# Decode attention over two layers: K fetched by pairs of heads into alternating slots, one loop turn per pair

## Chip, cores and metric

The kernel runs on one core of one Trainium2 chip. The metric is device time in microseconds (us) of one launch. TensorE is called PE, VectorE DVE, ScalarE ACT, GpSimd POOL and SyncE SP, as in the profile.

## What is computed

One token for each of two sequences (B = 2) passes two layers, each an attention over cached K and V and a gated mixer with an MLP. The attention is nearly all of the work:

```python
q = (x @ wq).reshape(B, Sq, H, Dh)                       # H = 32 heads, Dh = 128
scores = einsum("bhqd,bhkd->bhqk", q, k_cache) * Dh**-0.5 # Sk = 16384 keys per head
p = softmax(scores)
o = einsum("bhqk,bhkd->bhqd", p, v_cache)
x = x + o.reshape(B, Sq, H * Dh) @ wo
```

All arrays are bf16. K and V of one head are 4 MB each; there are U = 64 heads (B times H), and both layers read all of them. The last heads of layer 0 (61 to 63) stay on chip and come first in layer 1.

## The kernel before

**Memory.** SBUF holds one tensor `mem` of six slots, each 32768 bytes in each of 128 partitions: one slot for K or V of a head. `plan_all` (L516) writes down, in order, every transfer and the slot it goes to. SP issues them strictly in that order (L99 to L101): a transfer waits until the last readers of its slot are done, and all that stand behind it wait with it.

**The loop.** Most heads go in pairs through a hardware loop on PE, ACT and DVE: heads 1 to 60 in layer 0, 58 heads in layer 1 (`ENTER`, `LEAVE`, L347). K of the pair's first head has a slot, K of the second another, and V of both is one transfer into two neighbouring slots (`plan_pair`, L445), whose row is 65536 bytes for each partition. K comes in rows of 32768 bytes. In layer 0 two of the six slots are not used while the loop runs.

**One head.** A head's K lies as 128 blocks of 128 keys. Half of them are scored on PE: `transposes` (L1292) turns eight blocks (a chunk) into PSUM `tps`, ACT copies the chunk to `kt` (`evacuate`, L1310), and `scores` (L1317) multiplies it with the column of q. PE does the scores two chunks behind the transposes. The other half is scored on DVE: `dots` (L1340) multiplies 16 blocks with a row of q spread over the partitions and sums (L1348, L1354). Softmax takes the maximum on DVE, over the partitions by POOL's `partition_all_reduce` (L1370), and exp on ACT (L1382, L1385).

**A pair.** V of a pair puts head 0 on partitions 0 to 63 and head 1 on 64 to 127, but p of each head lies on all 128. So `spread_p` (L1407) redistributes p of each head by two matmuls, ACT copies the halves to `both` (L1424), and `pv_pair` (L1445) runs 256 matmuls with two columns each (L1455). Within one turn the order is: first head, second head with the softmax of the first inside, softmax of the second, PV of both, ACT's copy of the result to `o_acc` (L1459).

**Tokens.** That a transfer has landed is told to PE and DVE by POOL, in its own order (`relay`, L81; emitted at L205), between its reductions.

Of the kernel before, what the change touches and what calls it, by code (L numbers as in the profile page):

```python
# [32 lines left out]
class Graph:  # L33
# [10 lines left out]
    def __init__(self, nc):  # L44
        self.nc = nc
        self.ops = {e: [] for e in self.ENGS}
        self.all = []
        self.writer = {}
        self.readers = {}
        self.dma_sems = {}  # L50
        self.dma_count = {}
        self.loops = {e: {} for e in self.LOOPED}

# [55 lines left out]
    def loop(self, first, turns):  # L109

        for e, i in first.items():
            n = len(self.ops[e]) - i
# [21 lines left out]
    def emit(self):  # L134
# [76 lines left out]
        def runner(e):  # L211
            def run(eng):
# [3 lines left out]
                while i < len(ops):  # L216
                    if i in self.loops.get(e, ()):
                        n, turns = self.loops[e][i]
                        taken = self._turn(eng, ops, i, n, turns, taken, wait, needs, emit_op, handle)
# [15 lines left out]
    def _turn(self, eng, ops, first, n, turns, taken, wait, needs, emit_op, handle):  # L235
# [22 lines left out]
        with self.nc.Fori(0, turns, 1, engines=OrderedEngineSet([me]), head_slot={me: 0}) as turn:  # L258
            seen = {}
            for i in range(n):  # L260
# [3 lines left out]
            for k, v in step.items():  # L264
                eng.sem_inc(handle(k), -v)
        return {**taken, **{k: taken.get(k, 0) + v * turns for k, v in step.items()}}
# [65 lines left out]
class KB:  # L332
    NL = 2
    CH = 8
# [12 lines left out]
    ENTER = (1, 3)  # L347
    LEAVE = (61, 61)
# [28 lines left out]
    def _alloc(self):  # L377
# [14 lines left out]
        self.both_keys = [("qb", 0), ("p", 0), ("p2", 0), "both"]  # L392
        self.s_dve = [sb(f"s_dve{i}", [128, 2 * (self.BP - self.PB)], FP32) for i in range(self.NS)]
        self.q_f = sb("q_f", [128, U], FP32)
        self.q_col = sb("q_col", [128, self.NS], BF16)
        self.mx = sb("mx", [128, 5, self.NS], FP32)
        self.ls = sb("ls", [128, 2, self.NS], FP32)
        self.l = sb("l", [128, U], FP32)
# [46 lines left out]
    def plan_pair(self, u, slot):  # L445

        v = self.V.rearrange("b h s d -> (b h s d)")
        n = self.NB * 128 * 128
        self.store.plan(("w", u, 0, 2 * self.NB), "pair", slot * self.TILE, 2 * self.TILE,
                        [(lambda m: m, v[u * n:(u + 2) * n].rearrange("(p x) -> p x", p=128))])  # L450

# [64 lines left out]
    def plan_all(self):  # L516
# [10 lines left out]
        self.plan_tile("k", 0, 1)  # L527
# [5 lines left out]
        for t, u, slot in (("k", third, 1), ("k", third + 1, 3), ("v", third, 4), ("k", third + 2, 5),  # L533
                           ("v", third + 1, 0), ("v", third + 2, 2)):
# [22 lines left out]
        o, a, z = self.order(1), self.ENTER[1], self.LEAVE[1]  # L557
        assert a == self.CARRY + 1 and z == U - 3
        for s in range(a, z, 2):
            self.plan_tile("k", o[s], 3, (quarter, half, half + quarter) if s == a else ())  # L560
            self.plan_tile("k", o[s + 1], 5)
            if s == a:
                self.plan_tile("k", o[z], 0)
            self.plan_pair(o[s], 1)
        self.plan_tile("k", o[z + 1], 4)
        self.plan_tile("k", o[z + 2], 3)
        self.plan_tile("v", o[z], 5)
        self.plan_tile("v", o[z + 1], 1)
        self.plan_tile("v", o[z + 2], 2, (half,))
        self.cuts["wo", 1] = [(i, j, 4 * T + i * row) for i, j in ((0, 11), (11, 22), (22, 32))]  # L570
        at = 4 * T + 32 * row
        ats = [at, at + w3r, at + 2 * w3r, 0, w3r]
        assert at + 3 * w3r <= 6 * T
        w4_at = w3r + w3r // 2
# [3 lines left out]
        assert w4_at + 16 * row <= T and w1_at + 5 * row <= 4 * T  # L578
# [31 lines left out]
    def build(self):  # L610
# [8 lines left out]
        self.pool(lambda e: e.memset(self.both[:, 1, :], 0.0), writes=["both"])  # L619
# [354 lines left out]
    def attention(self, l):  # L974
        U, LEAD, NS = self.U, self.LEAD, self.NS
        self.l_now = l
        o = self.order(l)
        pend = []
        enter, leave = self.ENTER[l], self.LEAVE[l]
        turns = (leave - enter) // 2  # L980
# [601 lines left out]
```

## Time and profile before

| | us |
|---|---|
| median of three runs (2546.06 to 2546.59) | 2546.34 |
| the profiled execution, whole | 2545.75 |
| its span, first to last instruction | 2543.9 |
| DVE busy | 1875.3 |
| PE busy | 1588.5 |
| ACT busy | 1250.8 |
| HBM read | 1092.37 MB, 429 GB/s over the span |

The slices of the page give each engine's busy share and the DMA engines' in 40 equal pieces of the span; the chain follows the work that ended last back to what released it. A row of waits names who waited, for whom, how long in total, how often and the longest. Instructions that only set registers, branch or change semaphores are not counted as busy; they are shown when a line is asked for, with a q behind the engine's name.

### The profile page before, as it was taken

The numbers are of one execution on the slowest core, as the hardware profiler recorded it, in microseconds if no ns is written. First come the engines' busy times: TensorE is split into PE (matmuls) and PEld (weight loads), VectorE is DVE, ScalarE is ACT, GpSimd is POOL, SyncE is SP. The second block draws the span as 40 slices with busy tenths as digits, with TensorE's granted clock in tenths as the row PEclk, the third lists the DMA queues.
The fourth block names the chain that finished last, engine by engine and source line by source line (L and its number), as shares of the span: only waits on it lengthen the run. The fifth ranks groups of instructions, "written<-read, shape, count | busy, mean of one in ns | idle before, by whom it ended". The sixth has DMA issues, their size and how long they took to land.

```text
span 2543.9 us, 75560 instructions
## 1 busy us (share of the span) xinstructions
PE 1588.5 (62%) x34642; PEld 1520.1 (60%) x34642; DVE 1875.3 (74%) x1811; ACT 1250.8 (49%) x2114; POOL 109.6 (4%) x154
## 2 busy tenths in 40 slices
PE   3656666566566566565776656656656666566566
PEld 3555656566565565565765656656556566566566
DVE  5787787777877877877748687787787787777884
ACT  3454555554544544545535455454454555554553
POOL 0000000000000000000000000000000000000000
PEclk8666665565656656666656566566666565665665
DMA  9999999999999999999999999999999999999999
GB/s 414 424 437 429 434 438 430 428 442 424 434 433 432 432 437 428 436 435 426 418 413 432 434 429 437 429 431 439 425 435 433 431 436 433 428 437 430 432 431 383
DMA packets 38432, 1093.19 MB, mean 430 GB/s; under 512 B 4196, under 2 KB 5352, under 8 KB 11496
## 3 DMA queue, kind: packets, MB, share of 16 engines
q1 hardware_dynamic: 38376, 1092.39, 99.9%
q8 instruction: 41, 0.67, 0.1%
q14 instruction: 15, 0.12, 0.0%
HBM read 1092.37 MB, written 0.00 MB: 429 GB/s over the span
## 4 chain that ended last, share of the span: by engine, by line
DMA 60%; DVE 27%; PE 7%; issue 4%; ACT 1%; POOL 0%; SPq 0%; POOLq 0%; DVEq 0%; ACTq 0%
DMA mem<-in_A_k_cache_dram 57%; DVE s_dve L1354 17%; DVE prod L1348 9%; PE tps L1298 3%; DMA mem<-in_B_w_dram 1%; DMA mem<-in_A_v_cache_dram 1%; PE mps L1482 1%; PE sps L1328 1%; PE sps L1263 1%; DVE diag L1259 1%; ACT mem L1314 0%; PE mps L897 0%; PE mps L1455 0%; DMA mem<-in_A_wq_dram 0%; DMA mem<-in_A_wo_dram 0%
## 5 line engine op out<-in xcount | busy, mean ns | idle before, releaser
L1354 DVE TENSOR_REDUCE s_dve<-prod 128x16 f32<-128x2048 bf16 x504 | 1151.1, 2284 | 13.3
L1314 ACT ACTIVATE kt<-tps 128x1024 bf16<-128x1024 bf16 x992 | 966.5, 1029 | 171.8 <-PE tps L1298 159.9
L1348 DVE TENSOR_TENSOR prod<-mem,qb 128x2048 bf16<-128x2048 bf16 x492 | 602.1, 1224 | 524.5 <-POOLq L205 490.6
L1298 PE MATMUL tps<-same,mem 128*128 128x128 bf16 x8192 | 910.7, 285 | 31.3 <-issue 24.6
L1298 PEld LDWEIGHTS tps<-same,mem 128*128 128x128 bf16 x8192 | 730.8, 130 | 37.2 <-issue 30.2
L1455 PEld LDWEIGHTS mps<-both,mem 128*128 128x128 bf16 x15104 | 407.5, 103 | 48.2 <-ACT both L1424 43.2
L1455 PE MATMUL mps<-both,mem 128*128 128x2 bf16 x15104 | 412.5, 165 | 32.6 <-ACT both L1424 27.8
L1328 PE MATMUL sps<-q_col,kt 128*128 128x1 bf16 x7936 | 364.6, 168 | 53.6 <-ACT kt L1314 44.9
L1328 PEld LDWEIGHTS sps<-q_col,kt 128*128 128x128 bf16 x7936 | 351.7, 108 | 74.2 <-ACT kt L1314 69.6
L1418 PE MATMUL sps<-p,same 128*128 128x128 bf16 x236 | 46.3, 299 | 481.2 <-ACT p L1385 481.2
L1418 PEld LDWEIGHTS sps<-p,same 128*128 128x128 bf16 x236 | 15.6, 111 | 491.2 <-ACT p L1385 491.2
L1263 PE MATMUL sps<-diag,same 128*128 128x128 bf16 x126 | 36.0, 286 | 286.4 <-DVE diag L1259 284.6
L1370 POOL PARTITION_ALL_REDUCE mx<-mx x128 | 106.5, 832 | 2366.3 <-DVE mx L1368 2259.0
L1459 ACT ACTIVATE o_acc<-mps 128x2 f32 x59 | 10.2, 172 | 383.7 <-PE mps L1455 383.7
L1263 PEld LDWEIGHTS sps<-diag,same 128*128 128x128 bf16 x126 | 13.1, 104 | 296.8 <-DVE diag L1259 290.1
L1379 ACT ACTIVATE mx<-mx 128x1 f32<-128x1 f32 x128 | 26.2, 205 | 332.1 <-POOL mx L1370 332.0
L1266 ACT ACTIVATE qb<-sps 128x128 bf16<-128x128 f32 x123 | 33.8, 275 | 228.1 <-PE sps L1263 228.1
L1424 ACT ACTIVATE both<-sps 64x256 bf16<-64x256 f32 x118 | 44.6, 378 | 57.2 <-PE sps L1418 57.2
L1365 DVE TENSOR_REDUCE mx<-sps 128x1 f32<-128x64 f32 x128 | 28.2, 220 | 23.2 <-PE sps L1328 23.1
L1382 ACT ACTIVATE p<-s_dve,mx 128x64 bf16<-128x64 f32 x123 | 42.8, 348 | 4.0
L1314 ACT ACTIVATE mem<-tps 128x1024 bf16<-128x1024 bf16 x32 | 31.3, 1044 | 18.1 <-PE tps L1298 16.0
L1430 ACT ACTIVATE l<-ls 128x1 f32 (+1 forms) x120 | 35.3, 294 | 9.0
(131 smaller groups left out, 460.5 us busy)
## 6 DMA issues: line engine op xcount, KB each, us to landing
mem<-in_A_k_cache_dram SPq DMA_DIRECT2D x124, 4096.0 KB, 24.0
mem<-in_A_v_cache_dram SPq DMA_DIRECT2D x5, 4096.0 KB, 29.7
mem<-in_B_w_dram SPq DMA_DIRECT2D x21, 576.0 KB, 7.8
mem<-in_B_w_dram SPq DMA_DIRECT2D x7, 1152.0 KB, 32.7
mem<-in_A_v_cache_dram SPq DMA_DIRECT2D x3, 2048.0 KB, 36.9
mem<-in_A_wq_dram SPq DMA_DIRECT2D x10, 512.0 KB, 6.5
mem<-in_A_wo_dram SPq DMA_DIRECT2D x8, 576.0 KB, 18.4
mem<-in_A_wq_dram SPq DMA_DIRECT2D x4, 1024.0 KB, 8.0
```

Source lines behind the costliest of these rows:

```text
L1263: self.pe(lambda pe: pe.matmul(qps, lhsT=self.ones_bf[:, :], rhs=self.diag[:, :], start=True, stop=True, skip_group_check=True), reads=["o ...
L1298: ins = pe.transpose(self.tps[t][:, j * 128:(j + 1) * 128], buf[:, j * 128:(j + 1) * 128], self.ident[:, :])
L1314: self.act(lambda e: e.activation(out=out, in_=self.tps[t][:, :], func=ACT.Copy), reads=[("tps", t)], writes=keys, sig=("evac", c, t, k))
L1328: ins = pe.matmul(self.sps[sp][:, c * self.CH + j:c * self.CH + j + 1], lhsT=buf[:, j * 128:(j + 1) * 128], rhs=self.q_col[:, sp:sp + 1], ...
L1348: self.dv(lambda e: e.tensor_tensor(out=prod, in0=buf.rearrange("p (j d) -> p j d", d=128), in1=qbc, op=ALU.mult), reads=[("qb", r)] + key ...
L1354: self.dv(lambda e: e.tensor_reduce(out=sd[:, c0:c0 + DB], in_=prod, axis=AX.X, op=ALU.add), reads=["prod"], writes=[("s_dve", r)], sig=(" ...
L1370: self.pool(lambda e: e.partition_all_reduce(mx[3], mx[2], channels=128, reduce_op=ROP.max), reads=[("mx2", i), "cleared"], writes=[("mx3" ...
L1382: self.act(lambda e: e.activation(out=p[:, n:self.NB], in_=self.s_dve[i][:, 0:self.NB - n], func=ACT.Exp, bias=mx[4], scale=self.scale, ac ...
L1418: ins = pe.matmul(out[:, h * n:(h + 1) * n], lhsT=lhsT, rhs=self.p[i][:, :], start=True, stop=True, skip_group_check=True)
L1424: self.act(lambda e: e.activation(out=self.both[lo:hi, k, :], in_=out[lo:hi, :], func=ACT.Copy), reads=[("sps", 0), ("qps", 0)], writes=se ...
L1430: self.act(lambda e, c: e.activation(out=self.l[:, bass.ds(c, 1)], in_=self.ls[:, 0, i:i + 1], func=ACT.Identity, bias=self.ls[:, 1, i:i + ...
L1455: ins = pe.matmul(self.mps[:, 448:450], lhsT=buf[:, b * 128:(b + 1) * 128], rhs=self.both[:, :, col], start=b == 0, stop=b == 2 * self.NB ...
```

## The change

K of a pair is now one transfer like V, `kk`, into two neighbouring slots, alternately at two places: slots 0 and 1 or 2 and 3 in layer 0, slots 0 and 1 or 4 and 5 in layer 1 (`KK`). V of a pair, `vv`, has one place: slots 4 and 5, or 2 and 3. All six slots are in use. With K and V of a pair in one layout, both heads' K stands on its own half of the partitions throughout: scores have two columns, one max and one reduction serve both heads, and exp is written by four activations, each on 64 partitions, right where PV reads it; `spread_p` goes. PV of a pair is done one turn later, behind the scores of the next pair. A turn of the loop is one pair at one of the two places, so within the loop PE and DVE compute the place from the turn (`moved`). The first pair of each layer is written out ahead of the loop. Layer 1 enters the loop's heads one later (`ENTER` 4), so that one single head goes ahead of them, with its PV, and two come behind.

```diff
@@ class Graph, _turn
+            self.moved = (turn + 1) % 2 * self.shift[eng_name][first]
@@ class KB
-    ENTER = (1, 3)
-    LEAVE = (61, 61)
+    ENTER = (1, 4)
+    LEAVE = (61, 62)
+    KK = ((0, 2), (0, 4))
+    VV = (4, 2)
+    def plan_pairs(self, l):
+        o = self.order(l)
+        firsts = [o[s] for s in range(self.ENTER[l], self.LEAVE[l], 2)]
+        for i, u in enumerate(firsts):
+            self.plan_pair("kk", u, self.KK[l][i % 2])
+            if i:
+                self.plan_pair("vv", firsts[i - 1], self.VV[l])
+        return firsts[-1]
@@ plan_all
-        for u in range(1, third, 2):
-            self.plan_tile("k", u, 0)
-            self.plan_tile("k", u + 1, 2)
-            self.plan_pair(u, 4)
+        last = self.plan_pairs(0)
+        self.plan_tile("k", third, 1)
+        self.plan_pair("vv", last, self.VV[0])
...
+        s = self.ENTER[1] - 1
+        self.plan_tile("k", o[s], 3, (quarter, half, half + quarter))
+        self.plan_tile("v", o[s], 2)
+        last = self.plan_pairs(1)
@@ attention
+        self.single(l, s, ahead)
+        self.softmax_max(l, s, o[s])
+        self.softmax_exp(l, s, o[s])
+        self.landed(l, "v", o[s])
+        for g in range(4):
+            self.pv(l, s, o[s], g)
+        self.keep_by_act(l, s)
+        self.pool(lambda e: e.memset(self.both[64:, 0, :], 0.0), writes=[*self.both_keys, "cleared"])
+        firsts = [o[s] for s in range(enter, leave, 2)]
+        for i, u in enumerate(firsts):
+            if i == 1:
+                first = self.g.mark()
+                self.base = self.chunk
+            self.pair(l, i, u, firsts[i - 1] if i else None)
+        a, z = self.KK[l]
+        self.g.loop(first, len(firsts) - 1, (z - a) * self.TILE // 2)
@@ new
+    def pair(self, l, i, u, was):
+        n, CH, DB, NB = 4 * self.PB // self.CH, self.CH, self.DB, self.NB
+        nm = ("kk", u, 0, 2 * NB)
+        buf, keys = self.store.buf(nm), self.store.keys(nm)
+        base = self.KK[l][0] * self.TILE // 2
+        self.g.relay("tensor", keys, [("landed", nm)])
+        self.g.relay("vector", keys, [("seen", nm)])
...
+        def place(b, m):
+            if self.g.moved is None:
+                return buf[:, b * 128:(b + m) * 128]
+            return self.mem[:, bass.ds(self.g.moved + (base + b * 128), m * 128)]
...
+                    ins = pe.transpose(self.tps[t][:, j * 128:(j + 1) * 128], place(c * CH + j, 1), self.ident[:, :])
...
+                    ins = pe.matmul(self.sps[0][:, 2 * b:2 * b + 2], lhsT=kt[:, j * 128:(j + 1) * 128],
+                                    rhs=self.q_col2[:, :], start=True, stop=True, skip_group_check=True)
...
+        for c in range(n):
+            turned(c, self.chunk)
+            self.evacuate(c, self.chunk)
+            pend.append((c, self.chunk))
+            self.chunk += 1
+            while len(pend) > self.LEAD:
+                score(*pend.pop(0))
+            if c % 2 == 0:
+                dot(c // 2)
+            if c == n // 2 and was is not None:
+                self.pair_l(was)
+        while pend:
+            score(*pend.pop(0))
+        if was is not None:
+            self.pair_pv(was)
+        self.pair_q(keys)
+        self.used(l, nm, 2 * NB)
...
+        self.pool(lambda e: e.partition_all_reduce(self.mx2[:, 4:6], self.mx2[:, 2:4], channels=128, reduce_op=ROP.max),
+                  reads=["mx2_2", "cleared"], writes=["mx2_4"])
+        self.pair_column(u + 2)
...
+        for part in (1, 0):
+            for h, (lo, hi) in enumerate(sides):
+                src = self.s_dve2[lo:hi, :] if part else self.half_scores(h)
+                self.act(lambda e, h=h, lo=lo, hi=hi, src=src, part=part: e.activation(
+                    out=self.both[lo:hi, h, NB * part:NB * (part + 1)], in_=src, func=ACT.Exp,
...
+    def pair_pv(self, u):
+        nm = ("vv", u, 0, 2 * self.NB)
+        buf, keys = self.store.buf(nm), self.store.keys(nm)
+        self.g.relay("tensor", keys, [("landed", nm)])
+        n = 2 * self.NB // 4
+        for g in range(4):
+            def f(pe, g=g):
+                for b in range(g * n, (g + 1) * n):
+                    ins = pe.matmul(self.mps[:, 448:450], lhsT=buf[:, b * 128:(b + 1) * 128], rhs=self.both[:, :, b],
+                                    start=b == 0, stop=b == 2 * self.NB - 1, skip_group_check=True)
+                return ins
+            self.pe(f, reads=self.both_keys + [("landed", nm)] + keys, writes=["ops"], sig=("w", g))
+        self.act(lambda e, c: e.activation(out=self.o_acc[:, bass.ds(c, 2)], in_=self.mps[:, 448:450], func=ACT.Copy),
+                 reads=["ops"] + keys, writes=["o_acc"], sig="keep_pair", col=u)
+        self.used(0, nm, 2 * self.NB)
```

`single` does one head as the code before did, without a loop; `pair_q`, `pair_diag` and `pair_column` make the rows and columns of q for the next pair, and `pair_l` keeps the sums of exp.

Two places of the order. SP at the start of the program before, from K and V of head 0 on; 128x16384 is one head, 128x32768 a pair, and the wait is for the readers of the slot (PE is `done_tensor`, ACT `done_scalar`):

```order
L101 DMA mem<-in_A_k_cache_dram 128x16384
L101 DMA mem<-in_A_v_cache_dram 128x16384
L101 DMA mem<-in_A_k_cache_dram 128x16384 x2
L101 DMA mem<-in_A_v_cache_dram 128x32768 [waits done_tensor]
L101 DMA mem<-in_A_k_cache_dram 128x16384 [waits done_tensor] x2
L101 DMA mem<-in_A_v_cache_dram 128x32768 [waits done_scalar]
```

The same place of SP's queue now:

```order
L103 DMA mem<-in_A_k_cache_dram 128x16384
L103 DMA mem<-in_A_v_cache_dram 128x16384
L103 DMA mem<-in_A_k_cache_dram 128x32768
L103 DMA mem<-in_A_k_cache_dram 128x32768 [waits done_tensor]
L103 DMA mem<-in_A_v_cache_dram 128x32768
L103 DMA mem<-in_A_k_cache_dram 128x32768 [waits done_tensor]
L103 DMA mem<-in_A_v_cache_dram 128x32768 [waits done_scalar]
```

The first V pair has moved behind the second K pair, and from then on each K pair stands ahead of the V pair of the pair before it.

PE in a turn of the loop of layer 0 before, from its entry; `tps<-same,mem` are transposes, `sps<-q_col,kt` scores, L258 is the loop's own line:

```order
L258 UNCONDITIONAL_BRANCH
L1298 MATMUL tps<-same,mem 128x128 [waits landed_tensor_tensor]
L1298 MATMUL tps<-same,mem 128x128 x23
L1328 MATMUL sps<-q_col,kt 128x1 [waits scalar_tensor]
L1328 MATMUL sps<-q_col,kt 128x1 x7
L1298 MATMUL tps<-same,mem 128x128 x8
```

PE at the end of a turn of the same loop now, from the middle of its last chunk (ISA is a register instruction, L1260 is PV, `sps<-diag` and `sps<-p` spread the next rows of q):

```order
L1142 ISA
L1142 MATMUL tps<-same,mem 128x128
L1153 MATMUL sps<-q_col,kt 128x2 [waits scalar_tensor]
L1153 MATMUL sps<-q_col,kt 128x2 x7
L1153 MATMUL sps<-q_col,kt 128x2 [waits scalar_tensor]
L1153 MATMUL sps<-q_col,kt 128x2 x7
L1153 MATMUL sps<-q_col,kt 128x2 [waits scalar_tensor]
L1153 MATMUL sps<-q_col,kt 128x2 x7
L1260 MATMUL mps<-both,mem 128x2 [waits landed_tensor_tensor]
L1260 MATMUL mps<-both,mem 128x2 x255
L1228 MATMUL sps<-diag,same 128x128 [waits vector_tensor]
L1228 MATMUL sps<-p,same 128x128
```

Each transpose inside the loop now has a register instruction ahead of it, and PV stands behind the scores of the next pair instead of its own.

More of the change, by code (lines that the diff above doesn't have):

```diff
@@ L233, in emit, with _turn @@
                     sect(runner(e))
-    def _turn(self, eng, ops, first, n, turns, taken, wait, needs, emit_op, handle):
+    def _turn(self, eng, eng_name, ops, first, n, turns, taken, wait, needs, emit_op, handle):
         table = [[needs(ops[first + t * n + i]) for i in range(n)] for t in range(turns)]
@@ L1245, in landed @@
             self.g.relay("tensor", keys, [("landed", nm) for nm in some])
-            if both:
-                self.g.relay("vector", keys, [("seen", nm) for nm in some])
     def q_column(self, u, s):
@@ L1253, in q_column, with q_row @@
                 reads=["q_f"], writes=[("q_col", i)], sig=("qc", i), col=u)
-    def q_row(self, u, s, bank=None, ahead=False):
+    def q_row(self, u, s, bank=None, after=()):
         i = self.ix(self.l_now, s)
```

357 lines of the change are left out of this document (181 added, 176 removed).

## The prediction

> **What bounds the kernel now.** I read the page first: its slices, its DMA part and its chain.
>
> ```profile
> span 2543.9 us, 75560 instructions
> PE 1588.5 (62%) x34642; PEld 1520.1 (60%) x34642; DVE 1875.3 (74%) x1811; ACT 1250.8 (49%) x2114; POOL 109.6 (4%) x154
> DMA  9999999999999999999999999999999999999999
> q1 hardware_dynamic: 38376, 1092.39, 99.9%
> DMA 60%; DVE 27%; PE 7%; issue 4%; ACT 1%; POOL 0%; SPq 0%; POOLq 0%; DVEq 0%; ACTq 0%
> ```
>
> No engine is over 74%, and the transfers fill every slice: they take 99.9% of the span. The DVE share of the chain is therefore no bound by itself; it is what stands between two transfers of one slot. Next I read a turn of the loop, and a long stretch of turns, in the table by windows.
>
> ```profile
> 411.00:449.80 38.80, 23.57 (x521) 22.62 (x519) 29.29 (x27) 19.27 (x34) 1.66 (x2) 0.63 1.00 432
> 500.00:1100.00 600.00, 376.40 (x8141) 362.03 (x8140) 448.58 (x401) 299.88 (x512) 25.30 (x31) 0.61 1.00 432
> ```
>
> A pair of heads is 16.78 MB and takes 38.8 us at a DMA share of 1.00. So a pair of K or of V is 19.4 us, and one head's K or V is 9.7 us. Last, what SP waits for before it may issue:
>
> ```profile
> SPq L101 <- PE sps L1328: 1577.9, 120, 41.9
> SPq L101 <- ACT o_acc L1459: 683.3, 59, 37.5
> ...
> 410.95 15.15 SPq L101 DMA_DIRECT2D mem<-in_A_k_cache_dram  x2
> 437.17 0.33 SPq L101 DMA_DIRECT2D mem<-in_A_v_cache_dram  x1
> ```
>
> Every issue waits for a slot, yet early enough that the queue never empties. Hence two questions: does the change shorten the transfers, and can the queue still not run dry?
>
> **Part 1: longer rows.** The trace before has no K row of 64 KB, but it has stretches with other rows. First 500 to 1100 us, then 1276 to 1300 us (weights):
>
> ```profile
> DMA packets 6737, 259.08 MB, mean 432 GB/s; under 512 B 752, under 2 KB 752, under 8 KB 752
> ...
> DMA packets 2564, 9.82 MB, mean 409 GB/s; under 512 B 284, under 2 KB 284, under 8 KB 2560
> ```
>
> Without the small packets (the semaphores' writes) a row is 43.3 KB at 27.0 B/ns on each of 16 engines (1603 ns), and 4.3 KB at 25.6 B/ns (168 ns). Two equations give 10 ns per row, whatever its length. K of a pair falls from 256 rows to 128, so 8 rows fewer on each engine, 0.08 us, and one completion fewer, 0.01: 0.09 us per pair, and over 59 pairs **-5.3 us**. The bounds are 0 and, if the small rows understate it, twice that.
>
> [...]
>
> **Part 2: what the loop turn costs PE.** Of a turn, exp on half the partitions, scores with two columns and one max for both heads have near rows and lie beside the transfers. What has no row is the register instruction ahead of each of the 128 transposes (the slot alternates, so the address is computed). Its nearest rows are one turn's register step and branch on PE, and fused register instructions on ACT and DVE beside single ones there:
>
> ```profile
> L258 PEldq ALU_OP  x1: 36/36/36, 436.7 to 436.7; - x1
> L258 PEldq COMPARE_BRANCH  x1: 208/208/208, 436.8 to 436.8; - x1
> ...
> L1430 ACTq FUSED_REGOPS  x118: 46/52/60, 82.4 to 2457.7; - x118
> L1259 DVEq FUSED_REGOPS  x118: 65/67/75, 61.1 to 2450.5; - x118
> ...
> L258 DVEq ALU_OP  x59: 45/45/58, 80.6 to 2455.2; - x59
> L258 ACTq ALU_OP  x59: 35/35/35, 92.8 to 2464.7; - x59
> ...
> 429.86 6.99 PE L1455 MATMUL mps<-both,mem 128*128 128x2 bf16 x256 [0.47 <-ACT both L1424]
> 437.07 2.48 PEld L1298 LDWEIGHTS tps<-same,mem 128*128 128x128 bf16 x24 [0.31 <-issue]
> 438.14 6.54 ACT L1314 ACTIVATE kt<-tps 128x1024 bf16<-128x1024 bf16 x7 [1.00 <-PE tps L1298]
> ```
>
> The low end is PE's own 36 ns; the high end is half of the 310 ns in which PE takes a step and a branch at the turn's edge, 155 ns. I take **120 ns**: fused costs 1.5 times single on ACT and DVE, so 54 ns on PE, and from the step's start to the branch PE needs about 100 ns, 64 more than the step itself. A weight load with its matmul takes 27 ns (6.99 us by 256). Eight transposes then take 8 x 147 ns = 1.18 us, eight scores 0.22: **1.39 us a chunk**, over ACT's pace of 0.93 to 1.03 us for its copy, which was the pace before. Sixteen chunks: 22.3 us.
>
> From the landing of a pair's K to the first byte of the next V pair: 0.1 (token), 22.3, 0.7 (last copy, last scores), 7.0 (PV, which frees the V slots), 0.4 (ACT's copy), and 1.6 from issue to first byte, from these rows (the first issue, and the stretch in which bytes first move):
>
> ```profile
> 0.80 0.41 SPq L101 DMA_DIRECT2D mem<-in_A_wq_dram  x1
> ...
> 2.40:6.00 3.60, 0.00 (x0) 0.00 (x0) 0.00 (x0) 0.00 (x0) 0.00 (x0) 1.00 0.93 381
> ```
>
> That is 32.1 us. After that landing the queue still holds V of the pair before and K of the pair after, 38.8 us. In the steady loop **the queue does not run dry**, with 6.7 us left. Behind SP's wait for the V slots stands the issue of the next K, which nothing can overtake.
>
> **Part 3: where the queue does run dry.** The V slots are the only ones without a second place, and three places have less than 38.8 us behind them or a later start.
>
> ```profile
> 4.63 22.79 DMA mem<-in_A_k_cache_dram
> 30.11 2.30 DVE s_dve L1354
> 33.70 2.30 DVE s_dve L1354
> ...
> 27.51 1.04 PE L1298 MATMUL tps<-same,mem 128*128 128x128 bf16 x8 [4.24 <-POOLq L205]
> ...
> 45.40 3.58 PE L1482 MATMUL mps<-both,mem 128*128 128x1 bf16 x128 [8.29 <-ACT both L1385]
> ...
> L258 DVEq MOVE  x2: 36/40/43, 43.7 to 50.2; - x2
> L258 ACTq MOVE  x2: 34/34/35, 49.0 to 54.5; - x2
> ...
> L258 PEldq COMPARE_BRANCH  x1: 3642/3642/3642, 48.5 to 48.5; - x1
> ...
> L1365 DVE TENSOR_REDUCE mx<-sps 128x1 f32<-128x64 f32 x128 | 28.2, 220 | 23.2 <-PE sps L1328 23.1
> L1370 POOL PARTITION_ALL_REDUCE mx<-mx x128 | 106.5, 832 | 2366.3 <-DVE mx L1368 2259.0
> L1382 ACT ACTIVATE p<-s_dve,mx 128x64 bf16<-128x64 f32 x123 | 42.8, 348 | 4.0
> ...
> 44.87 0.19 ACT L1382 ACTIVATION_READ_ACCUMULATOR both<-s_dve,mx 128x1 f32 x1
> ```
>
> (a) The first turn of layer 0. Head 0's K lands at 27.4, its PV ends at 49.0; the queue holds V0 and the first K pair to 56.5, so the second K pair goes out in time. Landings: 56.5 (K pair 1), 75.9 (K pair 2), 95.3 (V pair 1), 114.7 (K pair 3). Pair 1 is not in the loop: eight dot products at 3.58 us (30.11 to 33.70) from 56.6 end, with two diagonals, at 85.6; five small operations for the maxima (0.22 each) and POOL's reduction (0.83, and 0.3 of hand-over) give 87.8. Only then does POOL, in order, tell of K pair 2. ACT's scale and four exps (0.35 and an accumulator read of 0.19 each) end at 90.3, and ACT enters its loop, which took 5.4 us before (49.0 to 54.5; DVE 6.5, PE 3.6): 95.7. PE has three chunks done and waits for the first copy, 96.7; 13 chunks at 1.39 are 18.1, then 0.7, PV 7.0, 0.4 and 1.6: 124.5. The queue was empty at 114.7: **9.8 us**.
>
> (b) The last turn of layer 0. Behind the last K pair the queue holds one V pair and one single K, 29.1 us, against 32.1: **3.0 us**.
>
> (c) The first turn of layer 1.
>
> ```profile
> 1343.57 1.23 PE mps L1482 x40
> 1344.80 4.97 issue
> ...
> 1357.25 19.14 DMA mem<-in_A_k_cache_dram
> ```
>
> Now a single head goes ahead of the pairs, and its softmax and PV are waited for. The head before it is done at 1344.8; a single head takes 21.5 (27.5 to 49.0 above): 1366.3, with memset and token 1366.7. Pair 1 takes 31.3 (56.6 to 87.9): 1398.0. The same 36.6 as in (a) to the first byte (87.9 to 124.5): 1434.6. The transfer landing at 1376.4 is the second loop K of before; back over K, a V pair and two K (48.5) the single head's K ended at 1327.9. Behind it now stand V (9.7), two K pairs, a V pair and a K pair (77.6): the queue is empty at 1415.2. **19.4 us**.
>
> Sum: 9.8 + 3.0 + 19.4 - 5.3 = +26.9. The execution shown took 2545.75 us against a span of 2543.9; +26.9 gives 2572.65. The runs' median lies 0.6 above that execution: **2573 us**.
>
> [...]
>
> **Rivals.** (1) Forecast: paced by the register instruction, three dry places; 36 to 155 ns give 2560 to 2588. 56%. (2) The register instruction hides behind ACT's copies: 1.03 us a chunk. (a) becomes 9.8 - 13 x 0.36 = 5.1, (b) 0, (c) 14.7; less 5.3 that is +14.5, 2560 us; without the loop entries' 5.4 twice, 2550. For it speaks that PE was paced by ACT; against it that PE takes instructions in order. 20%. (3) PE becomes the bound of every turn: it decides from (38.8 - 9.8) / 16 = 1.81 us a chunk, 172 ns a register instruction; each 10 ns beyond costs 1.28 us in each of 57 turns, 73 us, so 200 ns would give some 2790. Against it stands that it lies over my high end. 14%. (4) **Faster**: the dry places are covered and only the rows count, 2545.75 - 5.3 = 2540 us. It decides if the single head of layer 1 runs 20 us earlier beside the carried ones, so that (c) closes. Against it: its tokens stand in POOL's order behind the third head's reduction. 5%. That K isn't fetched in longer rows at all is excluded by V, which is already asked for in that shape. The last 5% is dry places that sum to about the gain, near 2546.
>
> About 0.2% (5 us) is what a measurement here tells from no change. Faster by more: 0.05. Within: 0.06 (the last case and a little of 2). Slower: 0.89. The range is 2550 to 2600: it holds cases 1 and 2 and the first step of 3, and leaves out the rest, 0.2.
>
> **What would show it.** Right: DMA slices of 9 with three dips, near 115, 1200 and 1420 us (the last two some 10 us later by then), each with SP waiting for ACT's copy of o; PE in a turn at about 1.4 us a chunk, turns still 38.7 us. Wrong: turns over 39 us with PE without idle time (3); eight transposes under 0.9 us (2); no SP wait over 35 us at the third place (4); a rate of 432 GB/s unchanged in the loop would cancel part 1.

## The result, and the profile after

The changed kernel takes 2564.4 us (median of four runs, 2562.1 to 2565.9) against 2546.2 us of the kernel before: a ratio of 1.0071, with a 95% interval of 1.0053 to 1.0088. It is 18 us slower. The forecast was 2573, in a range of 2550 to 2600. A later set of runs gave 2563.7 and 1.0063 (1.0047 to 1.0080).

The page of the changed kernel, those lines that were shown of before:

```profile
span 2564.1 us, 82334 instructions
PE 1646.0 (64%) x34410; PEld 1441.1 (56%) x34410; DVE 1903.5 (74%) x1697; ACT 1229.4 (48%) x1943; POOL 31.4 (1%) x97
DMA  9899999999999999999999899999999999999999
q1 hardware_dynamic: 29880, 1092.39, 99.0%
DMA 73%; PE 18%; issue 6%; ACT 1%; SPq 1%; another core or an unknown queue 0%; DVE 0%; POOL 0%; ACTq 0%; POOLq 0%
```

Two slices of the DMA row fell from 9 to 8, the second and the twenty-third (a slice is 64.1 us, so 64 to 128 and 1410 to 1474 us). All others are as full as before; the third dip that was forecast, near 1200 us, does not show in a slice. The number of packets fell by 8496, 7552 of them rows of K. DVE, with 27% of the chain before, has gone from it, and PE has 18% instead of 7%: PV now stands in every turn between the landing of one V pair and the issue of the next.

The table by windows of the changed kernel: a long stretch of turns, then the two open places (the last columns are PE's granted clock, DMA share and GB/s).

```profile
500.00:1100.00 600.00, 383.37 (x7813) 332.27 (x7813) 457.64 (x375) 295.38 (x468) 5.67 (x16) 0.67 1.00 433
112.80:123.00 10.20, 9.15 (x292) 8.53 (x288) 7.14 (x12) 2.71 (x8) 0.35 (x1) 0.50 0.29 93
1424.70:1436.00 11.30, 9.38 (x300) 8.71 (x299) 10.65 (x9) 2.74 (x6) 0.00 (x0) 0.55 0.28 91
```

The loop runs at 433 GB/s (432 before). In the two places it is 93 and 91: that is place (a), 10.2 us, and place (c), 11.3 us. As dry counts, here and below, the time in which fewer than some 13 to 14 of the 16 DMA engines have a packet under way. Place (b), near 1197 us, is 0.7 us by the packets of the trace; 1.6 more come at 1403.5 us, ahead of (c), and 1.7 among the mixer's weights at 1273, where nothing was forecast. Together 25.5 us.

What a turn takes is read from ACT's copy of o, once per pair, between 200 and 1150 us. The kernel before, and the changed one:

```profile
L1459 ACT ACTIVATE o_acc<-mps x25: 172/173/175, 204.3 to 1135.0; 128x2 f32 x25
```

```profile
L1264 ACT ACTIVATE o_acc<-mps x24: 172/173/174, 227.9 to 1118.4; 128x2 f32 x24
```

That is 930.7 us over 24 turns, 38.78 us, and 890.5 over 23, 38.72. A pair got 0.06 us shorter, 3.6 us over 59 pairs. So 25.5 us of dry queue less some 4 of shorter transfers is 21 to 22 us, against the 20.2 us by which the spans of the two profiles differ. By the packets of queue q1 the account closes: the time that the 16 engines spent on them fell from 2541.5 to 2538.6 us (99.9% and 99.0% of the spans), and what is left of the span grew from 2.4 to 25.5 us.

Whom SP waited for, in all and at most:

```profile
SPq L103 <- ACT o_acc L1264: 2106.5, 59, 37.9
SPq L103 <- PE sps L1228: 134.3, 57, 34.5
```

Most of the waiting is now for ACT's copy of o: V has one place, and this copy is the last that PV of the pair before needs of it.

### The profile page after: what moved, and what is told of

Same layout as the page of the kernel before. It is cut to its first block, busy times and chain, and to the rows that moved or that the text cites. A ratio compares the mean times of both kernels' runs of the same rounds, so it can differ in the third digit from the quotient of the medians.

```text
span 2564.1 us, 82334 instructions
## 1 busy us (share of the span) xinstructions
PE 1646.0 (64%) x34410; PEld 1441.1 (56%) x34410; DVE 1903.5 (74%) x1697; ACT 1229.4 (48%) x1943; POOL 31.4 (1%) x97
## 4 chain that ended last, share of the span: by engine, by line
DMA 73%; PE 18%; issue 6%; ACT 1%; SPq 1%; another core or an unknown queue 0%; DVE 0%; POOL 0%; ACTq 0%; POOLq 0%
DMA mem<-in_A_v_cache_dram 70%; PE mps L1260 16%; DMA mem<-in_B_w_dram 1%; SPq L103 1%; DMA mem<-in_A_k_cache_dram 1%; ACT kt L1466 1%; PE tps L1142 0%; ACT o_acc L1264 0%; PE mps L1588 0%; DMA mem<-in_A_wq_dram 0%; PE sps L1480 0%; DMA mem<-in_A_wo_dram 0%; PE tps L1451 0%; PE mps L919 0%
## 5 line engine op out<-in xcount | busy, mean ns | idle before, releaser
L1142 PE MATMUL tps<-same,mem 128*128 128x128 bf16 x7552 | 948.1, 244 | 575.7 <-POOLq L208 572.0
L1142 PEld LDWEIGHTS tps<-same,mem 128*128 (+1 forms) x7552 | 688.0, 99 | 745.5 <-issue 583.1
L1167 DVE TENSOR_REDUCE s_dve<-prod 128x16 f32<-128x2048 bf16 x472 | 1078.4, 2285 | 14.2
L1162 DVE TENSOR_TENSOR prod<-mem,qb 128x2048 bf16<-128x2048 bf16 x472 | 578.0, 1224 | 472.7 <-POOLq L208 412.5
L1260 PE MATMUL mps<-both,mem 128*128 128x2 bf16 x15104 | 412.2, 165 | 67.2 <-POOLq L208 62.2
L1260 PEld LDWEIGHTS mps<-both,mem 128*128 128x128 bf16 x15104 | 407.3, 103 | 72.1 <-POOLq L208 67.0
L1153 PE MATMUL sps<-q_col,kt 128*128 128x2 bf16 x7552 | 329.0, 165 | 46.6 <-ACT kt L1466 41.9
L1153 PEld LDWEIGHTS sps<-q_col,kt 128*128 128x128 bf16 x7552 | 289.9, 98 | 60.4 <-ACT kt L1466 46.3
L1264 ACT ACTIVATE o_acc<-mps 128x2 f32 (+1 forms) x59 | 10.2, 173 | 509.0 <-PE mps L1260 509.0
L1234 ACT ACTIVATE qb<-sps 64x128 bf16<-64x128 f32 x122 | 33.1, 272 | 123.2 <-PE sps L1228 121.2
L1451 PE MATMUL tps<-same,mem 128*128 128x128 bf16 x640 | 69.3, 284 | 11.4 <-POOLq L208 11.0
L1451 PEld LDWEIGHTS tps<-same,mem 128*128 128x128 bf16 x640 | 56.1, 130 | 11.8 <-POOLq L208 11.7
L1206 ACT ACTIVATE both<-s_dve,mx_ 64x128 bf16<-64x128 f32 x118 | 47.0, 399 | 2.7
L1206 ACT ACTIVATE both<-sps,mx_ 64x128 bf16<-64x128 f32 x118 | 42.8, 362 | 2.3
L1466 ACT ACTIVATE mem<-tps 128x1024 bf16<-128x1024 bf16 x32 | 31.1, 1047 | 19.4 <-PE tps L1451 17.1
L1247 ACT ACTIVATE l<-ls_ 64x1 f32 (+1 forms) x118 | 34.5, 292 | 9.0
```

What stands on the lines that cost most here:

```text
L1142: ins = pe.transpose(self.tps[t][:, j * 128:(j + 1) * 128], place(c * CH + j, 1), self.ident[:, :])
L1153: ins = pe.matmul(self.sps[0][:, 2 * b:2 * b + 2], lhsT=kt[:, j * 128:(j + 1) * 128], rhs=self.q_col2[:, :], start=True, stop=True, skip_g ...
L1162: self.dv(lambda e: e.tensor_tensor(out=prod, in0=place(NB + i * DB, DB).rearrange("p (j d) -> p j d", d=128), in1=qbc, op=ALU.mult), read ...
L1167: self.dv(lambda e: e.tensor_reduce(out=self.s_dve2[:, i * DB:(i + 1) * DB], in_=prod, axis=AX.X, op=ALU.add), reads=["prod"], writes=[("s ...
L1206: self.act(lambda e, h=h, lo=lo, hi=hi, src=src, part=part: e.activation(out=self.both[lo:hi, h, NB * part:NB * (part + 1)], in_=src, func ...
L1234: self.act(lambda e, h=h, lo=lo, hi=hi: e.activation(out=self.qb[1][lo:hi, :], in_=qps[lo:hi, 128 * h:128 * (h + 1)], func=ACT.Copy), read ...
```

## Experiments

Every time is a median; "before" was run beside each group, at 2546.9, 2547.5 and 2547.2 us.

### The control

The changed kernel again, without an edit, on the chip of the last three runs below.

> The changed kernel once more, unchanged, so that the next three runs have it on their own chip: 2564, a dry place of 10 us at 113 and one of 11 us at 1425.

2563.7 us, with 9.6 us dry in place (a) and 10.0 in (c). As expected.

### The length of rows

In `plan_pair`, K of a pair in pieces of the row (first run; the seventh uses 4):

```diff
+        src = v[u * n:(u + 2) * n].rearrange("(p x) -> p x", p=128)
+        w = 2 * self.NB * 128 // (2 if t == "kk" else 1)
...
-                        [(lambda m: m, v[u * n:(u + 2) * n].rearrange("(p x) -> p x", p=128))])
+                        [(lambda m, a=a: m[:, a:a + w], src[:, a:a + w]) for a in range(0, 2 * self.NB * 128, w)])
```

> The changed kernel, but each K pair comes as two transfers of 32768-byte rows, to the same places and behind the same semaphore. Theory A (a row costs some 10 ns whatever its length): 128 more rows per pair, 8 on each of the 16 engines, 0.08 us per pair plus one completion of 0.01; over 59 pairs 5.3 us more than the changed kernel, 2569.7 against 2564.4. The dry places stay. Theory B (the row length is worth nothing, the changed kernel is slower for its dry places alone): 2564.4, no change.

2567.2 us, ratio 1.0086 (1.0073 to 1.0100): 3 us over the changed kernel, but the runs of each spread over 4 to 5 us and were not made side by side. The direction is A's; the size was left to three more runs, side by side, in a kernel without large dry places (the fifth run, described further down).

> The fifth run with K of a pair as two transfers of 32768-byte rows: a kernel without dry places, where nothing but the rows differs. Theory A (10 ns a row and 10 ns a completion, as in the prediction): 5.3 us more than the fifth run. Theory B (row length is worth nothing): the same. Theory C (the first run gave 3 us over the changed kernel; part of a row's fixed time lies beside the next row): 3 us more.

> The fifth run with K of a pair as four transfers of 16384-byte rows: 24 more rows per engine and pair than with 64 KB. Theory A (10 ns a row, 10 ns a completion): 59 x (0.24 + 0.03) = 15.9 us more than the fifth run. Theory B: the same. Theory C (half of a row's fixed time hidden): 8 to 9 us more.

The fifth run took 2546.1 us, the sixth 2550.8, the seventh 2559.1: 4.8 and 13.0 us more, where A said 5.3 and 15.9. ACT's copy of o in the three, in the order of 64, 32 and 16 KB:

```profile
L1265 ACT ACTIVATE o_acc<-mps x25: 172/173/175, 220.3 to 1149.2; 128x2 f32 x25
```

```profile
L1267 ACT ACTIVATE o_acc<-mps x24: 172/173/175, 220.7 to 1112.6; 128x2 f32 x24
```

```profile
L1267 ACT ACTIVATE o_acc<-mps x24: 172/173/175, 221.4 to 1116.8; 128x2 f32 x24
```

A turn is 38.70, 38.78 and 38.93 us. The first halving costs 0.08 us per pair, the second 0.15, as it adds twice as many rows. Eight rows more per engine for 0.08 us are 10 ns a row, 24 for 0.23 also. A holds for the row; the 10 ns more for each completion, which are in its 15.9, don't show. The edits also make two and four transfers out of one, but the packets of the traces put the cost on the row: between 500 and 1100 us a row of 64, 32 and 16 KB took 2422, 1217 and 615 ns in the mean, so that the same bytes take some 12 ns more for each further row.

### When V's slots come free

The second run moves PV inside the turn:

```diff
+            if c == 8 and was is not None:
+                self.pair_pv(was)
         while pend:
             score(*pend.pop(0))
-        if was is not None:
-            self.pair_pv(was)
         self.pair_q(keys)
```

> The changed kernel, but PV of the pair before stands behind chunk 9 of 16 (index 8) in a turn instead of behind the last scores. Theory A (the V slots are released too late in the first turns, so SP stands and the queue runs dry): V is issued some 7 chunks of 1.05 us earlier, 7.4 us, and the stop of PE for instructions late in the first turn (1.6 and 1.4 us) no longer lies ahead of it. The dry place near 113 us (10 us) falls to 1 or 0, the one near 1425 us (11 us) to some 3: about 17 us less, 2547. Theory B (the queue isn't what is late, the time goes elsewhere): 2564, no change. Theory C (V of the steady loop lands 19.4 us behind K, so PE stands in the middle of each turn): a turn needs 19.4 + 7.0 + 7 x 1.05 + 3 = 37 us against 38.7 of transfers; it just fits, but if it does not, each us over costs 57 us.

2555.9 us, ratio 1.0037 (1.0023 to 1.0051): 8 us less, half of what A said, and no lateness in the steady loop, so C falls. Place (a) fell to 5.6 us and (c) to 6.6. PE in the first turn of layer 0 shows where the other half went:

```profile
103.56 2.55 PE L1260 MATMUL mps<-both,mem 128*128 128x2 bf16 x91
107.63 3.58 PE L1260 MATMUL mps<-both,mem 128*128 128x2 bf16 x128 [1.52 <-issue]
114.93 1.14 PE L1260 MATMUL mps<-both,mem 128*128 128x2 bf16 x37 [3.72 <-issue]
```

PV is cut in two places by stops that wait for nothing the profile knows, 1.5 and 3.7 us. They come once per layer, in the first turn of the loop (3.9 and 1.8 us in layer 1); between 500 and 1100 us PE has none. In the changed kernel the same 256 matmuls ran at 114.1 without a stop, while the transfer queue was empty. The traces' packets tell what PE stood for: in layer 0 packets of the instruction queue q8 landed at 106.33 and 113.65 us, and PE went on 1.3 us after each. Why they landed no earlier, no run here shows.

The third run takes two holds out of layer 1's start:

```diff
-        self.pool(lambda e: e.memset(self.both[64:, 0, :], 0.0), writes=[*self.both_keys, "cleared"])
...
-            if c == 0:
+            if c == (5 if l else 0):
                 ahead()
...
         self.g.relay("vector", keys, [("seen", nm)])
+        if was is None:
+            self.pool(lambda e: e.memset(self.both[64:, 0, :], 0.0), writes=[*self.both_keys, "cleared"])
```

> The changed kernel, but ahead of the pairs of layer 1 two things are put in another order: the rows of q for the pairs are made behind the single head's third dot product instead of ahead of its first (DVE stood 8.4 us there for PE), and POOL's memset of both stands behind its token for the first K pair instead of ahead of it (POOL stood 4.7 us there for the single head's PV). Theory A (place (c) of the prediction is the serial chain of the single head on DVE and POOL): the first pair starts some 6 to 8 us earlier, the dry place near 1425 us falls from 11 us to 3 to 5, 2557. Layer 0 stays as it is. Theory B (the chain isn't what V waits for there): 2564.

2558.5 us, ratio 1.0049 (1.0036 to 1.0063); A said 2557. The first pair's dot products start at 1366.2 instead of 1376.5, SP issues V at 1427.5 instead of 1434.7, the place before (c) is gone and (c) is 7.3 us. Place (a) stayed at 9.4.

The fourth run has the edits of the second and the third.

> Both edits together: PV behind chunk 9, and the single head of layer 1 without the two holds. Theory A (three dry places, and longer rows that gain 5 us): no place is dry for more than 1 us, so the time is that of the kernel before less the rows, 2546.2 - 5.3 = 2541, faster than before. Theory B (rows of 64 KB gain nothing): 2546. Theory C (something else in the changed kernel costs time in each turn): above 2546, with a turn over 38.8 us.

2550.1 us, ratio 1.0013 (1.0004 to 1.0022), not 2541. The trace still has 5.0 us dry in (a), behind the same two stops in PV, 1.6 in (c), 1.1 in (b) and 2.3 in the mixer. So neither B nor C is needed; A's "no more than 1 us" was wrong.

The fifth run is the fourth with PV ahead of the first scores (`c == 1` in place of `c == 8`), where PE stood idle for ACT.

> As the fourth run (PV inside the turn, the single head of layer 1 without its two holds), but PV stands behind the first two chunks of a turn, ahead of the first scores. In the first turn PE stood there for ACT's first copy, 5.9 us, and the stops for instructions that cut PV in two in the fourth run (2.1 and 3.7 us) come earlier with it. Theory A (only the dry queue counts): no dry place is left in front of a V pair, about 6 us less than the fourth run's 2550: 2544, below the kernel before (2547). Theory B (the fourth run stayed above the kernel before for another reason): 2550. Theory C (in the steady loop V lands 19.4 us behind K, and 7.0 + 14 x 1.05 us follow it, 41.1 in all against 38.7 of transfers; if the lateness adds up, 2.4 us in each of 57 turns): 2680. A says that it does not add up, since PE has 25 us of work in a turn.

2546.1 us, ratio 0.9995 (0.9986 to 1.0005): 4 us less than the fourth run, A's direction, and no different from the kernel before as far as can be measured. A's 2544 was 2 us too low. PE of the first turn:

```profile
97.05 6.30 PE L1261 MATMUL mps<-both,mem 128*128 128x2 bf16 x231 [7.77 <-POOLq L208]
107.90 0.83 PE L1261 MATMUL mps<-both,mem 128*128 128x2 bf16 x25 [4.55 <-issue]
```

The stop is still there, 4.6 us, but PV ends at 108.7, before the queue empties. (a) and (c) are gone from the trace. What remains dry is (b), now 2.7 us since PE's turns end later, and 1.7 us in the mixer: 4.4 of the 4.8 us that the rows bring. The steady turn is 38.70 us, so C falls here too.

### The register instruction

The eighth run has none: a turn of two pairs with fixed places.

```diff
-            if self.g.moved is None:
-                return buf[:, b * 128:(b + m) * 128]
-            return self.mem[:, bass.ds(self.g.moved + (base + b * 128), m * 128)]
+            return buf[:, b * 128:(b + m) * 128]
@@
-            if i == 1:
+            if i == 2 - l:
                 first = self.g.mark()
@@
-        self.g.loop(first, len(firsts) - 1, (z - a) * self.TILE // 2)
+        self.g.loop(first, (len(firsts) - 1) // 2, 0)
```

> The changed kernel without the register instructions: a turn of the loop is two pairs, one at each place, so that all addresses are fixed (layer 0 then has two pairs ahead of its loop, layer 1 one). Theory A (the register instruction makes a chunk 1.05 us on PE; without it ACT's copy paces it, 0.93): 13 chunks in each of the places (a) and (c), 1.6 us each, and in layer 0 the loop is entered one pair later, where 5 us of it are no longer ahead of V: 2556 to 2561. Theory B (the register instruction as in the prediction, 120 ns, 1.39 us a chunk): 6 us in each place, below 2552. Theory C (a turn of two pairs is twice the code, and fetching it in the first turn costs PE more than the register instructions): 2564 or above.

2607.6 us, ratio 1.0241 (1.0227 to 1.0255): 43 us slower than the changed kernel. C, and far more than C said. The instruction queue on the changed kernel's page, with packets, MB and share, and then on this one's:

```profile
q8 instruction: 49, 0.80, 0.1%
```

```profile
q8 instruction: 295, 4.83, 0.7%
```

PE at the end of PV inside a steady turn of the eighth run:

```profile
505.34 0.24 PE L1258 MATMUL mps<-both,mem 128*128 128x2 bf16 x3 [3.49 <-issue]
```

Its copies of o, and a long stretch of its loop in the table by windows:

```profile
L1262 ACT ACTIVATE o_acc<-mps x24: 172/173/174, 230.3 to 1139.3; 128x2 f32 x24
```

```profile
500.00:1100.00 600.00, 332.95 (x7782) 302.48 (x7779) 452.18 (x371) 274.84 (x450) 5.45 (x16) 0.64 1.00 425
```

246 more packets of instructions, over 28 turns of two pairs 8.8 a turn, and a pair now takes 39.52 us. The stops that the changed kernel has once per layer are here in every turn. Between 500 and 1101 us PE has 18 of more than 1 us that no semaphore ends, and each ends 1.2 to 1.6 us after a packet of queue q8 has landed. The transfer queue does not run dry for them in the loop (share 1.00); the 0.80 us more of a pair lie in the transfers. The instruction packets themselves are 0.7% of the engines' time, 0.28 us of a pair, and a row of 64 KB took 2448 ns in the mean instead of 2422, which is 0.42 us for the 256 rows of a pair on 16 engines; together that is most of the 0.80. Why the rows got longer is not shown.

A pair has 514 matmuls with their weight loads, 1028 instructions on PE; a turn of the changed kernel about 1160 with its register instructions, a turn of this one about 2060. Between 200 and 1150 us the trace of the changed kernel has no packet on that queue, the trace of this one 108, 9.0 a turn. No run has a turn of a length between these two.

The time of this run says nothing of the register instruction's price, since the longer code hides it. Its transposes do, a chunk at a granted clock of 0.99 (518.4 to 526.0 us) and one at 0.51 (556.0 to 559.5):

```profile
518.46 0.61 PE L1140 MATMUL tps<-same,mem 128*128 128x128 bf16 x8
518.91 0.34 PE L1151 MATMUL sps<-q_col,kt 128*128 128x2 bf16 x8
...
557.39 1.01 PE L1140 MATMUL tps<-same,mem 128*128 128x128 bf16 x8
558.20 0.40 PE L1151 MATMUL sps<-q_col,kt 128*128 128x2 bf16 x8
```

From the first transpose to the first score it is 0.45 and 0.81 us, 56 and 101 ns a transpose. In the first turn of the changed kernel, with the instruction, it is 0.86 us at a clock of 1.00 (from 103.57) and 0.81 at 0.50 (from 99.37). So the instruction costs some 51 ns per transpose at the full clock and nothing at half of it, and a chunk takes 1.04 to 1.07 us at either.

So two runs went the other way and made the instruction longer. The tenth:

```diff
-            return self.mem[:, bass.ds(self.g.moved + (base + b * 128), m * 128)]
+            at = self.g.moved + (base + b * 128)
+            if m == 1:
+                at = at * 3 // 3
+            return self.mem[:, bass.ds(at, m * 128)]
```

> The changed kernel with more arithmetic in the register instruction ahead of each transpose in the loop (the same address, multiplied by 3 and divided by 3 again). Theory A (the dry places are paced by PE's chunk, which was 1.05 us with 46 ns for this instruction): each ns more makes a chunk 8 ns longer, 13 chunks in the places (a) and (c), 0.1 us per ns in each, and (b) 0.13 us per ns beyond some 15 ns. With about 42 ns more a chunk takes 1.39 us, which is what the prediction assumed: +4.4, +4.4 and +3.4, 2576. Theory B (ACT's copy hides it, or the places do not hang on PE): 2564. The turn of the steady loop stays 38.7 us in both.

2577.9 us, ratio 1.0117 (1.0100 to 1.0134), 14.2 over the control. The register instructions by source line (ns, least, median and most), in the changed kernel and in the tenth run, and then PE in the first turn of the tenth run:

```profile
L1142 PEldq FUSED_REGOPS  x7296: 46/46/122, 87.5 to 2460.5; - x198
```

```profile
L1145 PEldq FUSED_REGOPS  x7296: 92/94/184, 87.4 to 2479.2; - x198
```

```profile
108.80 1.38 PE L1145 MATMUL tps<-same,mem 128*128 128x128 bf16 x8
109.97 0.40 PE L1156 MATMUL sps<-q_col,kt 128*128 128x2 bf16 x8
110.23 1.42 PE L1145 MATMUL tps<-same,mem 128*128 128x128 bf16 x8
```

The instruction grew from 46 to 94 ns and a chunk from 1.05 to 1.43 us: all 48 ns of each of eight transposes come through. For 48 ns A's rule gives 4.8 + 4.8 + 4.3 = 13.9 us, and 14.2 were measured; the dry places grew to 13.5, 5.4 and 15.6. B falls: nothing hides the 48 ns that were added. PE's granted clock was lower here (0.50 between 500 and 1100 us, 0.67 in the changed kernel), but that is not the cause: the changed kernel's chunk takes no longer at 0.50 (1.06 to 1.07 us from 98.31 to 101.50) than at 1.00 (1.04 to 1.06 from 103.57 to 107.77). The loop's turn stayed at 38.7.

The eleventh run has two such instructions (`(at * 3 // 3 + 7) * 5 // 5 - 7`).

> The changed kernel with two such register instructions ahead of each transpose, with two divisions in all. Theory A: as in the run before, by the length that the trace gives; from 1.81 us a chunk (38.8 us less 9.8, over 16 chunks; 95 ns more per transpose than in the changed kernel) PE becomes the bound of each turn and each 10 ns beyond cost 73 us. With 80 ns more: 2564 + 0.1 x 80 x 2 + 0.13 x 65 = 2588; with 120 ns more about 2600 + 180. Theory B (no such threshold, PE's lateness stays in the three places): below 2600 for any length up to 120 ns.

3339.7 us, ratio 1.3109 (1.3087 to 1.3131). PE in the loop, the loop's window, and the copies of o:

```profile
618.55 2.58 PE L1145 MATMUL tps<-same,mem 128*128 128x128 bf16 x8
...
621.20 2.60 PE L1145 MATMUL tps<-same,mem 128*128 128x128 bf16 x8
```

```profile
500.00:1100.00 600.00, 526.82 (x5930) 281.68 (x5928) 352.36 (x279) 229.99 (x353) 3.91 (x11) 0.50 0.77 327
```

```profile
L1267 ACT ACTIVATE o_acc<-mps x18: 172/173/174, 244.8 to 1124.5; 128x2 f32 x18
```

A chunk is 2.65 us, and the DMA share fell to 0.77 (1.00 in the changed kernel), with PE busy for 527 of the 600 us (383 there): PE is the bound. With the threshold of 1.81 us a turn should be (2.65 - 1.81) x 16 = 13.4 us over 38.7, 52.1; it is 51.75. A's threshold fits, and B, which had none, falls. The two instructions cost 200 ns more per transpose than the one, beyond the 120 that both theories had written out, and the threshold was tried from this one length only.

### The entry of the loop

```diff
-            if i == 1:
+            if i == 2:
                 first = self.g.mark()
@@
-            self.moved = (turn + 1) % 2 * self.shift[eng_name][first]
+            self.moved = turn % 2 * self.shift[eng_name][first]
```

(and one turn fewer in each loop)

> The changed kernel with two pairs written out ahead of the loop of each layer, so that the loop is entered one pair later. Theory A (the stops for instructions at the loop's entry, 5.5 us on ACT and 1.6 on PE in layer 0, 1.4 on PE in layer 1, and the register instructions are part of the dry places): the place at 113 us falls from 10 to about 1 us, but the next turn meets the same stops with little cover, some 5 us; the place at 1425 falls from 11 to 8. About 2557. Theory B (the stops come with any code that runs for the first time, in the loop or ahead of it): 2564. Theory C (more code ahead of the loop means more stops): above 2564.

2558.7 us, ratio 1.0043 (1.0026 to 1.0060), 5.1 below the control; A said 2557. The sum is near, the places are not: place (a) is 4.1 us where A had about 1, the next turn has none where A had 5, and (c) is 9.1 against 8. ACT and SP in the pair that is now written out:

```profile
89.84 8.36 ACT L1466 ACTIVATE kt<-tps 128x1024 bf16<-128x1024 bf16 x9
...
115.72 0.33 SPq L103 DMA_DIRECT2D mem<-in_A_v_cache_dram  x1
```

ACT goes on without its stop of 5.6 us, and V is issued 5.7 us earlier. A had the stops move to the next turn; ACT has none there. On PE, B is right in part: PV of the pair that is now written out still stops for 2.7 us, ahead of what is left of (a), and PV of the first turn in the loop for 0.6 and 3.7. Behind the latter no place is dry: a stop at a place with cover cost nothing.

## Why the prediction was right, and where a size was off

**What bounds the kernel.** Right: the loop stayed at full transfers, 433 GB/s and 38.7 us a turn, and all that was lost was lost where the queue ran dry.

**Part 1, longer rows, -5.3 us.** Right in kind and nearly in size: 4.8 us by the fifth and sixth run, 0.06 to 0.08 us per pair against 0.09. The 0.01 us that this sum has for a completion no run shows: in the sixth and seventh run 10 ns a row alone make up the 0.08 and 0.23 us.

**Part 2, the turn on PE.** Right that the steady queue would not run dry, and the threshold of 1.81 us stood its test. Right also that the register instruction would set PE's chunk, though only at the full clock. **The size was wrong**: the chunk was 1.05 us instead of 1.39. Two terms of that sum failed, in opposite directions. The register instruction was taken at 120 ns and measured 46; the 64 ns added from the branch at the turn's edge were the error, while the 54 ns from the comparison of fused with single instructions were nearly right. The 100 ns from the step to the branch there were not the price of a register instruction, 46 ns. And the transpose behind it was taken at 27 ns, read from PV's matmuls, which have 2 columns where a transpose has 128, though the prediction's own row at 27.51 us has eight transposes in 1.04 us; without a register instruction it took 56 ns at the full clock and 101 at half (eighth run). Together they were taken at 147 ns and came to 101 to 107. With 54 and 27 ns the sum would have given a chunk of 0.87 us, too low. The tenth run, with a chunk of 1.43 us, shows what the forecast's chunk would have cost: 2578.

**Part 3, the dry places: 9.8, 3.0 and 19.4 us forecast, 10.2, 0.7 and 11.3 measured.** The mechanism was right in all three: SP stands for ACT's copy of o. The first turn in layer 0 of the changed kernel, step by step:

```profile
87.69 3.23 PE L1142 MATMUL tps<-same,mem 128*128 128x128 bf16 x24 [3.23 <-POOLq L208]
...
95.72 8.88 ACT L1466 ACTIVATE kt<-tps 128x1024 bf16<-128x1024 bf16 x9 [5.62 <-issue]
96.88 0.35 PE L1153 MATMUL sps<-q_col,kt 128*128 128x2 bf16 x8 [5.97 <-ACT kt L1466]
...
103.57 1.02 PE L1142 MATMUL tps<-same,mem 128*128 128x128 bf16 x8
104.63 1.01 PE L1142 MATMUL tps<-same,mem 128*128 128x128 bf16 x8
...
110.25 0.23 PE L1142 MATMUL tps<-same,mem 128*128 128x128 bf16 x1 [1.64 <-issue]
114.13 6.97 PE L1260 MATMUL mps<-both,mem 128*128 128x2 bf16 x256
121.21 0.17 ACT L1264 ACTIVATE o_acc<-mps 128x2 f32 x1 [7.37 <-PE mps L1260]
121.41 0.33 SPq L103 DMA_DIRECT2D mem<-in_A_v_cache_dram  x1
```

POOL's token, ACT's entry (95.7 forecast, 95.72 measured; a packet on the instruction queue q14 landed 1.4 us before) and the first scores (96.7 and 96.88) came as written. Then 13 chunks took 4.4 us less, and a stop of 1.6 us and a slower end (ACT's last copies) took 2.9 back; the queue was empty 1.9 us sooner, at 112.8. Place (a) is thus right partly because two errors cancel.

In (c) they do not. The same engines in layer 1:

```profile
1403.64 0.33 SPq L103 DMA_DIRECT2D mem<-in_A_k_cache_dram  x1
1409.36 8.75 ACT L1466 ACTIVATE kt<-tps 128x1024 bf16<-128x1024 bf16 x9
1423.56 0.23 PE L1142 MATMUL tps<-same,mem 128*128 128x128 bf16 x1 [1.41 <-issue]
1434.71 0.33 SPq L103 DMA_DIRECT2D mem<-in_A_v_cache_dram  x1
```

ACT enters its loop here without a stop, where 5.4 us were forecast from layer 0; with the 4.4 us of the chunks and 1.4 of a stop on PE that is 8.4 less than 19.4: 11.0, and 11.3 were measured. At 1403.64 SP waited for a K slot, which the prediction did not see (1.6 us). In (b) sixteen chunks were 5.4 us shorter than forecast, more than its 3.0, and yet 0.7 us stayed dry. There the chunks no longer decide. PV waits there for POOL's token for its V (L208), which lands one transfer of a pair, 19.4 us, behind K, and the prediction's sum has no such wait:

```profile
1188.66 6.99 PE L1260 MATMUL mps<-both,mem 128*128 128x2 bf16 x256 [0.93 <-POOLq L208]
```

**The rivals.** The second one's 1.03 us a chunk came close by its number, and so did its 2560, and its reason holds in part. Its sign, eight transposes under 0.9 us, came too: 0.86 and 0.81 up to the first score. At the full clock a chunk takes PE 0.65 us without the instructions (0.45 and 0.20 in the eighth run) and 1.05 with them, while ACT's copy paces it at 0.92 there: 0.27 of the 0.40 us lie behind ACT, 0.13 don't, and of what the tenth run added nothing does. The third would have needed 172 ns by the prediction's sum, some 140 by the measured chunk; the eleventh run shows that beyond it the time does rise as priced. The fourth needed (c) closed by 20 us earlier work; the third run shows that 10 us earlier are worth 5 of time.

## What to carry to other kernels

When a kernel is bound by transfers, as this one is (a DMA share of 1.00 between 500 and 1100 us), a change is priced by what it does to the time between the last reader of a buffer and the next issue, and the first turn of a loop is the place to work it out: the steady turns lost nothing (38.72 us a pair against 38.78), and 22.2 of the 25.5 us of dry queue lay in (a), (b) and (c), where a loop began or ended. A buffer with a single place wants its last reader early in the turn. Moving PV (and two holds) brought back 18 us without touching a transfer, while the 64 KB rows themselves were worth 5.

## What the runs showed of the hardware

- A fused register instruction on PE took 46 ns, and 94 with a multiplication and a division in it. Ahead of a transpose the first one cost some 51 ns at a granted clock of 1.0 (107 ns a transpose instead of 56) and nothing at 0.5 (101 with and without); the 48 ns of the longer one came on top in full.
- Between 200 and 1150 us the eighth run's loop, whose turn has some 2060 instructions on PE, fetched 108 packets of 16 KB, 9.0 a turn; the changed kernel's, with 1160, fetched none. All 18 stops of PE over 1 us between 500 and 1101 us in the former ended 1.2 to 1.6 us after such a packet had landed. The rate of data there fell from 433 to 425 GB/s, though the packets took only 0.7% of the engines.
- A row of 64, 32 and 16 KB took a DMA engine 2422, 1217 and 615 ns in the mean between 500 and 1100 us, some 12 ns more for each further row of the same bytes; about 10 ns a row showed in the time of a turn.
- PE's granted clock was 0.61 in the loop before, 0.67 in the changed one and 0.50 in the tenth and eleventh run's (500 to 1100 us in each).
